# A softmax-weighted causal convolution and a squared-ReLU FFN: the convolution as masked band matmuls on TensorE instead of products on GpSimd and adds on VectorE

## The chip, the cores and the metric

One NeuronCore of a Trainium2 chip runs the whole program. The metric is the device time of one execution in microseconds (us). The engines are TensorE (PE, with its weight loads listed apart as PEld), VectorE (DVE), ScalarE (ACT), GpSimd (POOL) and SyncE (SP), which here only issues DMAs. Each engine takes its own instructions in its own order and waits on semaphores for the others.

## The reference

There are 8 batches of 4096 tokens with 192 channels. Each token has, for each of 8 heads, 7 weights; a softmax over the 7 makes them add up to one. A head owns 24 neighbouring channels, and output token s is the weighted sum of the input tokens s-6 to s (zeros ahead of the batch). The result goes through an FFN of 2048 hidden units.

```
w = exp(weight_gen - max);  w = w / sum(w)              # over the 7 taps
x_pad = 6 rows of zeros, then x                         # per batch
y[b,s,h,g] = sum_k  w[b,s,h,k] * x_pad[b, s+k, h, g]    # h: 8 heads, g: 24 channels
h = maximum(y @ w_in, 0)                                # 192 -> 2048
out = (h * h) @ w_out                                   # 2048 -> 192
```

Inputs and output are f32; inside, both kernels use f16 operands with f32 sums in TensorE.

## The kernel before

The 32768 tokens are cut into 64 blocks of 512 tokens (`TB`), a block into four chunks of 128 tokens, one token to a partition. The loop over `it` is a software pipeline: in one round block `it` loads its inputs, block `it-1` is convolved, block `it-2` transposed, block `it-3` does the first FFN product and block `it-4` the second. The order in which the instructions stand on each engine is set by the framework's scheduler from this program order and from its own estimates of readiness; the rows shown further down are that final order.

- **Load** (`st_dma_in`, L89 to L112, on SP's queue): the weights of the block, and for each chunk a tile `X6` that holds seven shifted copies of the 128 rows, in f32.
- **Softmax** (L117 on ACT, L121 and L124 on DVE, L129 on POOL).
- **Products** (`st_mult`, L140, POOL): one instruction per chunk multiplies the seven shifted copies by their tap weights into `pk`, 1344 elements on each of 128 partitions, f16. `pk` has two buffers, one for each block in flight.
- **Adds** (`st_preadd`, L152, L155, L158, DVE): the seven products are summed in three instructions per chunk.
- **Transposes** (`st_fold_pe`, L169, PE): eight per block turn the sums to channels-by-tokens; ACT copies them out (L179). The 192 channels are held as two groups of 128 that overlap by 64; the overlapping rows of `w_in` are zero in the second group. The first FFN product therefore has two matmuls for each 128 hidden units.
- **First FFN product** (`st_mm1`, L188, 32 matmuls of 128x512 per block), ReLU on ACT (`st_relu`, L204, into `t1`, four buffers), square on DVE (`st_sq`, L209).
- **Second FFN product** (`st_mm2`, L219, 64 matmuls of 192 columns per block), copied out by ACT (L230) and sent by SP (L237).

Of the kernel before, what the change touches and what calls it, by code (L numbers as in the profile page):

```python
# [7 lines left out]


@with_exitstack
def kernel(
# [7 lines left out]
):  # L20
    nc = tc.nc
# [3 lines left out]
    B, S, D = x.shape  # L25
    H, KK = weight_gen.shape[2], weight_gen.shape[3]
    G = D // H
    Dff = moe_w_in.shape[1]
    Dm = moe_w_out.shape[1]
    PAD = KK - 1  # L30
# [3 lines left out]
    NCH = TB // P  # L34
    NBLK_PER_B = S // TB
    NBLK = B * NBLK_PER_B
    NF = Dff // P
    NFP = NF // 2

# [4 lines left out]
    d_chunks = [(0, P), (D - P, P)]  # L44

    const = ctx.enter_context(tc.tile_pool(name="const", bufs=1))

    ident = const.tile([P, P], f16, name="ident")
    make_identity(nc, ident)

    w_in16 = []
    for ci, (dd0, dn) in enumerate(d_chunks):
        t = const.tile([P, Dff], f16, name=f"w_in16_{ci}")
        if ci == 0:
            nc.gpsimd.dma_start(out=t, in_=moe_w_in[dd0 : dd0 + P, :])
        else:
            pad = 2 * P - D
            nc.vector.memset(t[0:pad, :], 0.0)  # L58
            nc.gpsimd.dma_start(out=t[pad:P, :], in_=moe_w_in[dd0 + pad : D, :])
        w_in16.append(t)  # L60

    w_out16 = const.tile([P, NF, Dm], f16, name="w_out16")
    nc.gpsimd.dma_start(  # L63
        out=w_out16, in_=moe_w_out.rearrange("(c p) m -> p c m", p=P)
    )

    p_wg = ctx.enter_context(tc.tile_pool(name="p_wg", bufs=2))
    p_e = ctx.enter_context(tc.tile_pool(name="p_e", bufs=2))
    p_sm = ctx.enter_context(tc.tile_pool(name="p_sm", bufs=2))
    p_nrm = ctx.enter_context(tc.tile_pool(name="p_nrm", bufs=2))  # L70
    p_x6 = ctx.enter_context(tc.tile_pool(name="p_x6", bufs=3))
    p_pk = ctx.enter_context(tc.tile_pool(name="p_pk", bufs=2))
    p_yt = ctx.enter_context(tc.tile_pool(name="p_yt", bufs=2))
    p_t1 = ctx.enter_context(tc.tile_pool(name="p_t1", bufs=4))
    p_g = ctx.enter_context(tc.tile_pool(name="p_g", bufs=2))
    p_os = ctx.enter_context(tc.tile_pool(name="p_os", bufs=3))
    ps_y = ctx.enter_context(tc.tile_pool(name="ps_y", bufs=1, space=bass.MemoryType.PSUM))
    ps_h = ctx.enter_context(tc.tile_pool(name="ps_h", bufs=3, space=bass.MemoryType.PSUM))
    ps_o = ctx.enter_context(tc.tile_pool(name="ps_o", bufs=1, space=bass.MemoryType.PSUM))

    wg_t, e_t, rcp_t, nrm_t, x6_t, pk_t, yt_t, g_t = ({} for _ in range(8))
    t1_t, hps_t, o2_t, osb_t = ({} for _ in range(4))

    def st_dma_in(j):
        b = j // NBLK_PER_B
        t0 = (j % NBLK_PER_B) * TB
        wg = p_wg.tile([P, NCH, H, KK], f32, name="wg")
        wg_t[j] = wg
        nc.sync.dma_start(  # L89
            out=wg,  # L90
            in_=weight_gen[b, t0 : t0 + TB].rearrange("(c p) h k -> p c h k", p=P),
        )
        X6 = p_x6.tile([P, NCH, KK, D], f32, name="X6")
        x6_t[j] = X6
        for c in range(NCH):
            s0 = t0 + c * P
            if s0 == 0:
                nc.vector.memset(X6[0:PAD, c, 0:PAD, :], 0.0)  # L98
                for k in range(KK):
                    tstart = max(0, PAD - k)  # L100
                    nc.sync.dma_start(  # L101
                        out=X6[tstart:P, c, k, :],
                        in_=x[b, 0 : P - PAD + k, :],
                    )
            else:
                base = x[b, s0 - PAD : s0 - PAD + P, :]
                src = bass.AP(
                    tensor=base.tensor,
                    offset=base.offset,
                    ap=[list(base.ap[0]), [D, KK], list(base.ap[1])],  # L110
                )
                nc.sync.dma_start(out=X6[:, c], in_=src)  # L112

    def st_exp(j):
        e = p_e.tile([P, NCH, H, KK], f32, name="e")
        e_t[j] = e
        nc.scalar.activation(out=e, in_=wg_t[j], func=ActF.Exp)  # L117

    def st_sm(j):
        ssum = p_sm.tile([P, NCH, H], f32, name="ssum")  # L120
        nc.vector.tensor_reduce(out=ssum, in_=e_t[j], axis=AxisX, op=AluOp.add)  # L121
        rcp = p_sm.tile([P, NCH, H], f32, name="rcp")
        rcp_t[j] = rcp
        nc.vector.reciprocal(out=rcp, in_=ssum)  # L124

    def st_nrm(j):
        nrm = p_nrm.tile([P, NCH, H, KK], f32, name="nrm")
        nrm_t[j] = nrm
        nc.gpsimd.tensor_tensor(  # L129
            out=nrm,  # L130
            in0=e_t[j],
            in1=rcp_t[j].unsqueeze(-1).broadcast_to((P, NCH, H, KK)),
            op=AluOp.mult,
        )

    def st_mult(j, c):
        if c == 0:
            pk_t[j] = p_pk.tile([P, NCH, KK, H, G], f16, name="pk")
        pk = pk_t[j]
        nc.gpsimd.tensor_tensor(  # L140
            out=pk[:, c],
            in0=x6_t[j][:, c].rearrange("p k (h g) -> p k h g", h=H),
            in1=nrm_t[j][:, c]
            .rearrange("p h k -> p k h")
            .unsqueeze(-1)
            .broadcast_to((P, KK, H, G)),
            op=AluOp.mult,
        )

    def st_preadd(j, c):  # L150
        v = pk_t[j][:, c].rearrange("p k h g -> p k (h g)")
        nc.vector.tensor_tensor(  # L152
            out=v[:, 0:3, :], in0=v[:, 0:3, :], in1=v[:, 4:7, :], op=AluOp.add
        )
        nc.vector.tensor_tensor(  # L155
            out=v[:, 0:2, :], in0=v[:, 0:2, :], in1=v[:, 2:4, :], op=AluOp.add
        )
        nc.vector.tensor_tensor(  # L158
            out=v[:, 0], in0=v[:, 0], in1=v[:, 1], op=AluOp.add
        )  # L160

    def st_fold_pe(j):
        yps = ps_y.tile([P, 2, TB], f16, name="yps")
        yt_t[j] = [yps, None]
        pk = pk_t[j]
        for c in range(NCH):
            y16 = pk[:, c, 0].rearrange("p h g -> p (h g)")
            for ci, (dd0, dn) in enumerate(d_chunks):
                nc.tensor.transpose(  # L169
                    out=yps[:, ci, c * P : (c + 1) * P],  # L170
                    in_=y16[:, dd0 : dd0 + P],
                    identity=ident,
                )

    def st_yt_evac(j):
        yps = yt_t[j][0]
        yt16 = p_yt.tile([P, 2, TB], f16, name="yt16")
        yt_t[j][1] = yt16
        nc.scalar.copy(out=yt16, in_=yps)  # L179

    def st_mm1(j, fp):
        yt16 = yt_t[j][1]
        hps = ps_h.tile([P, 2, TB], f32, name="hps")
        hps_t[(j, fp)] = hps
        for jj in range(2):
            fc = 2 * fp + jj
            for ci, (dd0, dn) in enumerate(d_chunks):
                nc.tensor.matmul(  # L188
                    out=hps[:, jj, :],
                    lhsT=w_in16[ci][:, fc * P : (fc + 1) * P],  # L190
                    rhs=yt16[:, ci, :],
                    start=(ci == 0),
                    stop=(ci == len(d_chunks) - 1),
                )
# [119 lines left out]
```

## Time and profile before

| | |
|---|---|
| device time, median of 2 runs | 1389.86 us (1389.41 to 1390.3) |
| profiled execution, span from first to last instruction | 1387.2 us |
| PE busy / PEld busy | 937.2 us (68%) / 627.6 us (45%) |
| DVE busy | 1070.5 us (77%) |
| ACT busy | 632.5 us (46%) |
| POOL busy | 725.6 us (52%) |
| mean granted TensorE clock | 0.836 of full speed |
| 16 DMA engines, hardware queue q1 | 42.2% |

The profile gives one execution. Its span is 2.7 us shorter than the median of the runs, which also hold what lies ahead of the first and behind the last instruction. Busy shares are averages over the run. A row of the groups view reads: line, engine, operation, output<-input, sizes, count, then busy time and mean duration of one, then the idle time of the engine ahead of these instructions and who ended it. A row of the timeline reads: start, duration of the stretch, engine, line, operation, count, and in brackets the idle time ahead of it. Matmul durations overlap, since they are pipelined; the distance from one start to the next is what a matmul costs in a stream.

### The profile page before, as it was taken

How to read it: one execution, taken by the hardware profiler on the slowest of the kernel's cores; microseconds unless marked ns; L12 is line 12 of the kernel's file. 1: busy time of each engine (PE TensorE's matmuls, PEld its weight loads, DVE VectorE, ACT ScalarE, POOL GpSimd, SP SyncE). 2: the span in 40 equal slices, each digit the busy share in tenths (PEclk: the TensorE clock that was granted, in tenths of full speed). 3: DMA queues.
4: the chain of work that ended last, by engine and by line, in shares of the span. 5: the costliest groups of instructions: out<-in, count | busy, mean ns of one | idle time of the engine just before them, and what ended most of it. 6: DMA issues, size and time to landing. Idle time of an engine off the chain costs nothing.

```text
span 1387.2 us, 17548 instructions
## 1 busy us (share of the span) xinstructions
PE 937.2 (68%) x6656; PEld 627.6 (45%) x6656; DVE 1070.5 (77%) x1417; ACT 632.5 (46%) x769; POOL 725.6 (52%) x329
## 2 busy tenths in 40 slices
PE   0376666766766766767767668668667667677688
PEld 0144443544544544534535435435445445444456
DVE  2989778778787787787787787787887877877863
ACT  0244444544544544444444445445445445444455
POOL 3766545646546546456456455455465465464430
PEclk9888888878888888788788878888888888788899
DMA  8524456554443543444443443544434434434001
GB/s 240 218 101 153 144 194 242 192 176 143 159 179 120 173 177 128 166 143 144 181 161 129 166 167 139 183 149 140 177 137 158 176 119 177 173 107 179 15 24 41
DMA packets 114053, 211.26 MB, mean 152 GB/s; under 512 B 42264, under 2 KB 82032, under 8 KB 113968
## 3 DMA queue, kind: packets, MB, share of 16 engines
q1 hardware_dynamic: 111680, 208.57, 42.2%
q0 software_dynamic: 2288, 1.57, 0.8%
q8 instruction: 52, 0.85, 0.3%
q14 instruction: 33, 0.27, 0.1%
HBM read 186.52 MB, written 25.17 MB: 153 GB/s over the span
## 4 chain that ended last, share of the span: by engine, by line
DVE 52%; PE 25%; POOL 12%; ACT 6%; issue 3%; SPq 1%; DMA 1%; POOLq 0%; ACTq 0%; DVEq 0%
DVE pk L152 17%; DVE pk L155 16%; PE o L219 16%; DVE pk L158 13%; POOL pk L140 12%; PE hps L188 9%; DVE gT L209 5%; ACT t L204 4%; ACT o_sb L230 2%; SPq L112 1%; DMA wg<-in_weight_gen_dram 1%; SPq L101 1%; DVE ssum L121 0%; PE yps L169 0%; DVE rcp L124 0%
## 5 line engine op out<-in xcount | busy, mean ns | idle before, releaser
L140 POOL TENSOR_TENSOR pk<-X,nrm 128x1344 f16<-128x1344 f32 x256 | 672.1, 2655 | 511.5 <-ACT o_sb L230 469.0
L188 PE MATMUL hps<-yt,w_in 128*128 128x512 f16 x2048 | 526.3, 408 | 374.1 <-ACT t L204 373.0
L204 ACT ACTIVATE t<-hps 128x1024 f16<-128x1024 f32 x512 | 489.8, 1028 | 424.7 <-DVE gT L209 403.0
L188 PEld LDWEIGHTS <-w_in 128*128 128x128 f16 x2048 | 206.3, 101 | 620.7 <-issue 425.7
L152 DVE TENSOR_TENSOR pk<-pk 128x576 f16<-128x576 f16 x256 | 264.1, 1032 | 231.6 <-POOL pk L140 231.6
L219 PE MATMUL o<-w_out,gT 128*128 128x192 f16 x4096 | 421.3, 268 | 8.5 <-DVE gT L209 7.3
L219 PEld LDWEIGHTS <-gT 128*128 128x128 f16 x4096 | 395.3, 108 | 65.4 <-issue 45.4
L209 DVE TENSOR_TENSOR gT<-t 128x1024 f16<-128x1024 f16 x512 | 344.4, 711 | 28.3 <-ACT t L204 24.8
L155 DVE TENSOR_TENSOR pk<-pk 128x384 f16<-128x384 f16 x256 | 249.4, 974 | 6.3
L158 DVE TENSOR_TENSOR pk<-pk 128x192 f16<-128x192 f16 x256 | 207.5, 811 | 6.2
L230 ACT COPY o_sb<-o 128x384 f32<-128x384 f32 x128 | 61.2, 478 | 266.4 <-PE o L219 266.4
L129 POOL TENSOR_TENSOR nrm<-e,rcp 128x224 f32<-128x224 f32 x64 | 50.5, 789 | 91.8 <-DVE rcp L124 65.7
L169 PE MATMUL yps<-ident,pk 128*128 128x128 f16 x512 | 42.2, 222 | 63.9 <-DVE pk L158 63.9
L179 ACT COPY yt<-yps 128x1024 f16<-128x1024 f16 x64 | 64.8, 1012 | 31.6 <-PE yps L169 31.6
L169 PEld LDWEIGHTS <-pk 128*128 128x128 f16 x512 | 33.5, 98 | 69.8 <-POOL pk L140 59.0
L121 DVE TENSOR_REDUCE ssum<-e 128x32 f32<-128x224 f32 x64 | 24.2, 377 | 26.0 <-ACT e L117 26.0
L117 ACT ACTIVATE e<-wg 128x224 f32<-128x224 f32 x64 | 24.5, 383 | 28.3 <-DMA wg<-in_weight_gen_dram 28.3
L124 DVE RECIPROCAL rcp<-ssum 128x32 f32<-128x32 f32 x64 | 22.5, 352 | 5.3 <-DVE ssum L121 0.5
L98 DVE MEMSET X<- 6x1152 f32 x8 | 8.1, 1018 | 1.4 <-issue 1.2
L58 DVE MEMSET w_in<- 64x1024 uint32 x1 | 0.9, 912 | 1.0 <-PEq L298 1.0
L117 ACT ACT_TABLE_LOAD x1 | 1.3, 1283 | 0.7 <-PEq L298 0.7
L63 POOL DMA_DIRECT2D w_out<-in_moe_w_out_dram x1 | 1.2, 1208 | 0.0
(8 smaller groups left out, 2.2 us busy)
## 6 DMA issues: line engine op xcount, KB each, us to landing
X<-in_x_dram SPq DMA_DIRECT2D x248, 672.0 KB
out_dram<-o_sb SPq DMA_DIRECT2D x128, 192.0 KB
wg<-in_weight_gen_dram SPq DMA_DIRECT2D x64, 112.0 KB
X<-in_x_dram SPq DMA_DIRECT2D x8, 96.0 KB
w_out<-in_moe_w_out_dram POOLq DMA_DIRECT2D x1, 768.0 KB, 18.3
X<-in_x_dram SPq DMA_DIRECT2D x8, 95.2 KB
X<-in_x_dram SPq DMA_DIRECT2D x8, 94.5 KB
X<-in_x_dram SPq DMA_DIRECT2D x8, 93.8 KB
```

What stands on the lines that cost most here:

```text
L129: nc.gpsimd.tensor_tensor(out=nrm, in0=e_t[j], in1=rcp_t[j].unsqueeze(-1).broadcast_to((P, NCH, H, KK)), op=AluOp.mult,)
L140: nc.gpsimd.tensor_tensor(out=pk[:, c], in0=x6_t[j][:, c].rearrange("p k (h g) -> p k h g", h=H), in1=nrm_t[j][:, c] .rearrange("p h k -> ...
L152: nc.vector.tensor_tensor(out=v[:, 0:3, :], in0=v[:, 0:3, :], in1=v[:, 4:7, :], op=AluOp.add)
L155: nc.vector.tensor_tensor(out=v[:, 0:2, :], in0=v[:, 0:2, :], in1=v[:, 2:4, :], op=AluOp.add)
L158: nc.vector.tensor_tensor(out=v[:, 0], in0=v[:, 0], in1=v[:, 1], op=AluOp.add)
L169: nc.tensor.transpose(out=yps[:, ci, c * P : (c + 1) * P], in_=y16[:, dd0 : dd0 + P], identity=ident,)
L179: nc.scalar.copy(out=yt16, in_=yps)
L188: nc.tensor.matmul(out=hps[:, jj, :], lhsT=w_in16[ci][:, fc * P : (fc + 1) * P], rhs=yt16[:, ci, :], start=(ci == 0), stop=(ci == len(d_ch ...
L204: nc.scalar.activation(out=t1, in_=hps_t[(j, fp)], func=ActF.Relu)
L209: nc.vector.tensor_tensor(out=gT[:, 2 * fp : 2 * fp + 2, :], in0=t1, in1=t1, op=AluOp.mult)
L219: nc.tensor.matmul(out=o2[:, c % 2, :], lhsT=gT[:, fc, c * P : (c + 1) * P], rhs=w_out16[:, fc, :], start=(fc == 0), stop=(fc == NF - 1),)
L230: nc.scalar.copy(out=o_sb, in_=o2_t[(j, half)])
```

## The change

The convolution is rewritten, and with it everything ahead of the FFN. The work is still 64 blocks of 512 tokens.

- **Softmax by batch.** `st_wg_load` loads the weights of a whole batch in one tile, 32 tokens and a halo of 6 to a partition (2128 f32 per partition). `st_softmax` runs one exp on ACT (L135), one reduce (L137), one reciprocal (L139) and five multiplies (L147) on DVE, eight times in all. The multiplies write the rows skewed into one of two tiles `v0`, `v1` (`vbuf`; both are `v_...` in the rows below), so that token t's own 8 slots hold the weights that it takes in the outputs t to t+6. SP writes this to a DRAM tile `vd` (L155).
- **Loads.** For each block five overlapping windows of 128 tokens, 98 apart, are loaded: `xt` (x in f16, converted by the DMA, on POOL's queue) and `wr` (the skewed weights from `vd`, on SP's queue; 64 f16 a row).
- **Bands.** `st_band` (L200, DVE, five per block) multiplies `wr`, repeated along the free axis, by a constant 0/1 mask; the result `bd` is for each head a 128 by 96 to 112 band matrix.
- **Convolution.** `st_conv` (L228, PE) contracts `xt` (as weights) with `bd`: 16 matmuls per window, 80 per block. Each has all 128 rows and up to 32 columns of weights (`tile_position=(0, p0)`, one of four column groups), because a group of 32 channels touches two heads: first with the later head over all 32 channels, then again with the earlier head over its 8, 16 or 24 channels. The output `yp` is already channels-by-tokens. Channels 128 to 191 are written twice, to partitions 0 to 63 and 64 to 127.
- **FFN.** `y` is copied from PSUM by DVE (L241). The first product stays at two matmuls per 128 hidden units: `w_b`'s upper 64 rows are zero (`ROW_TILED` is False). `st_mm2` is issued in eight parts, one behind each of the eight pairs of `st_mm1`. `h` has two PSUM buffers (before: three), `o` two (before: one).
- **Gone:** `X6`, the products on POOL, the adds, the transposes, the identity.

```
+    def st_softmax(b):
+        wg = wg_t[b]
+        v = vbuf[b % 2]
+        nc.scalar.activation(out=wg, in_=wg, func=ActF.Exp)
+        ssum = p_sm.tile([P, RH, H], f32, name="ssum")
+        nc.vector.tensor_reduce(out=ssum, in_=wg, axis=AxisX, op=AluOp.add)
+        rcp = p_sm.tile([P, RH, H], f32, name="rcp")
+        nc.vector.reciprocal(out=rcp, in_=ssum)
+        pp = list(v.ap[0])
+        for i0 in range(0, RH, SL):
+            n = min(SL, RH - i0)
+            vo = bass.AP(
+                tensor=v.tensor, offset=v.offset + i0 * H * SL,
+                ap=[pp, [H * SL + 1, n], [SL, H], [H * SL, KK]],
+            )
+            nc.vector.tensor_tensor(
+                out=vo,
+                in0=wg[:, i0 : i0 + n],
+                in1=rcp[:, i0 : i0 + n].unsqueeze(-1).broadcast_to((P, n, H, KK)),
+                op=AluOp.mult,
+            )
+        vd = p_dr.tile([S, H * SL], f16, name="vd")
...
+    def st_band(j, i):
+        if i == 0:
+            bd_t[j] = p_bd.tile([P, H * TB], f16, name="bd")
+        lo, hi = bounds[i], bounds[i + 1]
+        n = hi - lo
...
+        nc.vector.tensor_tensor(
+            out=bd_t[j][:, H * lo : H * hi].rearrange("p (h m c) -> p h m c", h=H, c=SL),
+            in0=wr_t[j][:, i].unsqueeze(2).broadcast_to((P, H, n // SL, SL)),
+            in1=m.rearrange("p (m c) -> p m c", c=SL)
+            .unsqueeze(1)
+            .broadcast_to((P, H, n // SL, SL)),
+            op=AluOp.mult,
+        )
...
+    def st_conv(j):
+        yp = ps_y.tile([P, 2, TB], f32, name="yp")
...
+        for i in range(NT):
+            lo, hi = bounds[i], bounds[i + 1]
+            bd = bd_t[j][:, H * lo : H * hi].rearrange("p (h c) -> p h c", h=H)
+            for later in (True, False):
+                for q, ci, p0 in places:
+                    _, ha, hb, pre = quads[q]
+                    m = 32 if later else pre
+                    nc.tensor.matmul(
+                        out=yp[p0 : p0 + m, ci, lo:hi],
+                        lhsT=x_t[j][:, i, 32 * q : 32 * q + m],
+                        rhs=bd[:, hb if later else ha, :],
+                        start=True,
+                        stop=True,
+                        skip_group_check=True,
+                        tile_position=(0, p0),
                     )
...
+        st_softmax(0)
+        st_load(0)
+        load_weights()
+        st_load(1)
+        st_load(2)
+        for i in range(NT):
+            st_band(0, i)
+        st_conv(0)
+        st_y_evac(0)
+        for j in range(NBLK + 1):
+            nb = j // NBB + 1
+            if j < NBLK and nb < B:
+                if j % NBB == 0:
+                    st_wg_load(nb)
+                if j % NBB == 2:
+                    st_softmax(nb)
+            if j + 3 < NBLK:
+                st_load(j + 3)
+            for fp in range(NFP):
+                if j < NBLK:
+                    st_mm1(j, fp)
+                    st_relu(j, fp)
+                if j >= 1:
+                    st_mm2(j - 1, fp)
+                if j < NBLK:
+                    if j + 1 < NBLK:
+                        if fp < NT:
+                            st_band(j + 1, fp)
+                        if fp == NT:
+                            st_conv(j + 1)
+                            st_y_evac(j + 1)
+                    st_sq(j, fp)
```

How the instructions stand on PE. Before, in the middle of the run, the transposes of a block (L169, reading `pk`) stand between two halves of the second FFN product (L219) and the first matmul of the next block's first product (L188):

```order
L219 MATMUL o_5526<-w_out_68,gT 128x192
L169 LDWEIGHTS pk [waits Pool_49]
L169 MATMUL yps<-ident,pk 128x128
L169 LDWEIGHTS pk
L169 MATMUL yps<-ident,pk 128x128
```

Now, at the same point of a block, the last of the 80 convolution matmuls (L228) is followed directly by the next pair of the first product (L249 and L254); ahead of the convolution stands a part of the second product:

```order
L228 MATMUL yp<-bd,xt 8x112
L228 LDWEIGHTS xt
L228 MATMUL yp<-bd,xt 16x112
L228 LDWEIGHTS xt
L228 MATMUL yp<-bd,xt 8x112
L249 LDWEIGHTS w_a
L249 MATMUL h<-y,w_a 128x512 [waits Activation_49]
L254 LDWEIGHTS w_b
L254 MATMUL h<-y,w_b 128x512
```

The eight transposes are gone, 80 narrow matmuls with a weight load each have come, and the two FFN products alternate in eighths.

How they stand on DVE, in the middle of the run. Before, each chunk's three adds wait for POOL's product, and the squares (L209) stand among and behind them:

```order
L152 TENSOR_TENSOR pk<-pk 128x576 [waits Pool_49]
L209 TENSOR_TENSOR gT<-t_5637 128x1024 [waits Activation_49]
L155 TENSOR_TENSOR pk<-pk 128x384 [waits DVE_49]
L209 TENSOR_TENSOR gT<-t_5644 128x1024 [waits Activation_49]
L158 TENSOR_TENSOR pk<-pk 128x192 [waits DVE_49]
L209 TENSOR_TENSOR gT<-t_5656 128x1024 [waits Activation_49]
L209 TENSOR_TENSOR gT<-t_5664 128x1024 [waits Activation_49]
```

Now there is no wait for POOL; the copy of `yp` (L241) waits for the convolution of block j+1, and behind it come the bands (L200) of block j+2 and the last two squares (L279) of block j:

```order
L279 TENSOR_TENSOR g<-t_6073 128x1024 [waits Activation_49]
L241 CAST y<-yp 128x1024 [waits PE_49]
L200 TENSOR_TENSOR bd<-wr,mask 128x832 [waits DMAHW3_49,DVE_49]
L200 TENSOR_TENSOR bd<-wr,mask 128x832
L279 TENSOR_TENSOR g<-t_6172 128x1024 [waits Activation_49]
L200 TENSOR_TENSOR bd<-wr,mask 128x768 x2
L279 TENSOR_TENSOR g<-t_6188 128x1024 [waits Activation_49]
L200 TENSOR_TENSOR bd<-wr,mask 128x896
```

The scheduler has moved the bands a whole block ahead of the convolution that reads them.

At the start of the program DVE now begins with the softmaxes of the first two batches, interleaved (`v_101` is the first batch, `v_102` the second):

```order
L308 MEMSET v_101 128x1408
L308 MEMSET v_102 128x1408
L102 MEMSET w_b 64x1024
L137 TENSOR_REDUCE ssum<-wg 128x304 [waits DMAHW0_49,Activation_49]
L137 TENSOR_REDUCE ssum<-wg 128x304 [waits DMAHW1_49,Activation_49]
L139 RECIPROCAL rcp<-ssum 128x304 [waits DVE_49] x2
L147 TENSOR_TENSOR v_101<-wg,rcp 128x8x8x7 [waits DVE_49]
L147 TENSOR_TENSOR v_102<-wg,rcp 128x8x8x7 [waits DVE_49]
```

The softmax of the second batch, written in the third round of the loop, now stands ahead of the first band; those of the other six batches stand among the first ten or so blocks.

More of the change, by code (lines that the diff above doesn't have):

```diff
@@ L6 @@
 from concourse import bass_utils, mybir
-from concourse.masks import make_identity
 from concourse._compat import with_exitstack
+ROW_TILED = False
 @with_exitstack
@@ L114, in st_exp @@
[L114 to L132, printed above, removed]
+            out=vd.rearrange("(p r) c -> p (r c)", p=P),
@@ L162, in st_fold_pe @@
[L162 to L179, printed above, removed]
+    G = D // H
```

322 lines of the change are left out of this document (161 added, 161 removed).

## The prediction

> **What bounds the kernel now.** I read the page first (busy shares, slices, chain), then the timeline of one block in the middle, then the same lines at the end of the run.
>
> ```profile
> core 0: 1387.2 us, clock 0.836
> PE 937.2 (68%) x6656; PEld 627.6 (45%) x6656; DVE 1070.5 (77%) x1417; ACT 632.5 (46%) x769; POOL 725.6 (52%) x329
> DVE 52%; PE 25%; POOL 12%; ACT 6%; issue 3%; SPq 1%; DMA 1%; POOLq 0%; ACTq 0%; DVEq 0%
> L140 POOL TENSOR_TENSOR pk<-X,nrm 128x1344 f16<-128x1344 f32 x256 | 672.1, 2655 | 511.5 <-ACT o_sb L230 469.0
> ```
>
> No engine is full, and the chain is half DVE's. The timeline of one block in the middle shows why (start, duration, engine, line, count, idle time ahead):
>
> ```profile
> 605.72 10.45 POOL L140 TENSOR_TENSOR pk<-X,nrm 128x1344 f16<-128x1344 f32 x4 [9.56 <-ACT o_sb L230]
> 608.31 2.80 DVE L152 TENSOR_TENSOR pk<-pk 128x576 f16<-128x576 f16 x1 [4.05 <-POOL pk L140]
> 611.14 2.60 DVE L155 TENSOR_TENSOR pk<-pk 128x384 f16<-128x384 f16 x1
> 613.78 2.50 DVE L158 TENSOR_TENSOR pk<-pk 128x192 f16<-128x192 f16 x1
> 616.21 0.45 DVE L152 TENSOR_TENSOR pk<-pk 128x576 f16<-128x576 f16 x1
> 619.71 1.94 ACT L204 ACTIVATE t<-hps 128x1024 f16<-128x1024 f32 x2 [6.70 <-DVE gT L209]
> 620.41 0.25 DVE L158 TENSOR_TENSOR pk<-pk 128x192 f16<-128x192 f16 x1
> 620.79 1.86 PE L188 MATMUL hps<-yt,w_in 128*128 128x512 f16 x4 [6.40 <-ACT t L204]
> 621.78 3.62 DVE L209 TENSOR_TENSOR gT<-t 128x1024 f16<-128x1024 f16 x6
> 625.74 0.61 PE L169 MATMUL yps<-ident,pk 128*128 128x128 f16 x8
> 626.43 10.46 POOL L140 TENSOR_TENSOR pk<-X,nrm 128x1344 f16<-128x1344 f32 x4 [9.34 <-ACT o_sb L230]
> ```
>
> A block takes 626.43 - 605.72 = 20.7 us. While POOL multiplies, a DVE add lasts about as long as a POOL product: 2.80, 2.60 and 2.50 us, against 0.45 and 0.25 us for the same instructions once POOL has stopped at 616.2. Squares queue behind these adds, the ReLUs wait 6.70 us for `t1` buffers, PE waits 6.40 us for the ReLUs. POOL's next block then starts 0.08 us behind the end of the transposes that free its `pk` buffer (the bracket names an ACT copy that feeds no product). So the block's period is a ring through four engines.
>
> The ring does not bind at the end, where POOL is out of work. Windows there and in the middle (length, busy time by engine, granted clock, DMA share, GB/s), and the timeline:
>
> ```profile
> 600.00:700.00 100.00, 72.78 (x520) 48.82 (x519) 78.53 (x100) 48.11 (x59) 55.43 (x24) 0.83 0.43 151
> 1336.00:1376.00 40.00, 40.00 (x327) 28.38 (x326) 17.80 (x27) 28.15 (x34) 0.00 (x0) 0.99 0.10 31
> ...
> 1351.80 0.25 PE L219 MATMUL o<-w_out,gT 128*128 128x192 f16 x1
> 1352.33 0.38 PE L188 MATMUL hps<-yt,w_in 128*128 128x512 f16 x1
> 1352.61 2.80 PE L219 MATMUL o<-w_out,gT 128*128 128x192 f16 x32
> 1355.25 6.86 PE L188 MATMUL hps<-yt,w_in 128*128 128x512 f16 x31
> 1356.10 7.44 ACT L204 ACTIVATE t<-hps 128x1024 f16<-128x1024 f32 x8 [0.17 <-PE hps L188]
> ```
>
> With PE never idle the granted clock is 0.99; in the middle, with 6.4 us of idle per block, it is 0.83. So PE loses twice: the wait, and a slower clock behind it.
>
> **The change, part by part.** All of POOL's 672.1 us and the adds go, and with them the ring. What is late next? I compare the engines per block.
>
> *PE, FFN.* At full clock, start to start: a 512-column matmul (6.86 - 0.38)/30 = 0.216 us, a 192-column one (2.80 - 0.25)/31 = 0.082 us. So 32 x 0.216 + 64 x 0.082 = 6.91 + 5.27 = 12.2 us per block. The padding of K costs nothing new: there were two matmuls per 128 hidden units before.
>
> *PE, convolution.* 80 matmuls of 96 to 112 columns (mean 102.4) with 32 or fewer columns of weights. The trace has no such shape. The nearest row is the transposes of 128 columns:
>
> ```profile
> L169 PE MATMUL yps<-ident,pk 128*128 128x128 f16 x512 | 42.2, 222 | 63.9 <-DVE pk L158 63.9
> L169 PEld LDWEIGHTS <-pk 128*128 128x128 f16 x512 | 33.5, 98 | 69.8 <-POOL pk L140 59.0
> ```
>
> Eight in 0.61 us, the last lasting 0.22: (0.61 - 0.22)/7 = 0.056 us apart, each with a weight load of 98 ns hidden beside its neighbours. From 0.216 at 512 columns and 0.056 at 128, a column costs 0.417 ns; 102.4 columns then cost 0.045 us, and 80 of them **3.6 us** per block. Ends: the four column groups side by side, a quarter, 0.9 us; each matmul with an unhidden weight load, 0.045 + 0.098 = 0.143 us, 11.4 us. I take 3.6, since the transposes, also a load per matmul, lie on that line.
>
> The Trainium skill, "TensorEngine Tiling (Array Packing)", section "Key Properties", says that a change of tiling mode drains TensorE. No row here shows it. As an estimate by that page, two drains of some 0.16 us (0.22 - 0.056) per block would add about 21 us to the run.
>
> *PE in all:* 12.2 + 3.6 = **15.8 us** per block.
>
> *DVE.* The rows that price it, with those of ACT:
>
> ```profile
> L209 DVE TENSOR_TENSOR gT<-t 128x1024 f16<-128x1024 f16 x512 | 344.4, 711 | 28.3 <-ACT t L204 24.8
> L179 ACT COPY yt<-yps 128x1024 f16<-128x1024 f16 x64 | 64.8, 1012 | 31.6 <-PE yps L169 31.6
> L230 ACT COPY o_sb<-o 128x384 f32<-128x384 f32 x128 | 61.2, 478 | 266.4 <-PE o L219 266.4
> L121 DVE TENSOR_REDUCE ssum<-e 128x32 f32<-128x224 f32 x64 | 24.2, 377 | 26.0 <-ACT e L117 26.0
> L117 ACT ACTIVATE e<-wg 128x224 f32<-128x224 f32 x64 | 24.5, 383 | 28.3 <-DMA wg<-in_weight_gen_dram 28.3
> L124 DVE RECIPROCAL rcp<-ssum 128x32 f32<-128x32 f32 x64 | 22.5, 352 | 5.3 <-DVE ssum L121 0.5
> ```
>
> Squares, 8 x 3.62/6 = 4.8 us. The copy of `yp`, 1024 f32 from PSUM, was ACT's at 1.01 us; between 0.7 (L209) and 1.7 (L121 scaled up) I take 1.2. Bands: 4096 f16 elements in five instructions; from 0.25 us at 192 and 0.45 at 576, 832 cost 0.58, so 2.9 us; at worst twice that if the repeated operand halves the rate, 5.8. Sum 8.9, at worst 11.8, under PE's 15.8.
>
> Softmax, per batch: reduce of 2128 at most 9.5 x 0.377 = 3.6, I take 2.4 (part of 0.377 is fixed); reciprocal of 304 at most 9.5 x 0.352 = 3.3, I take 2.6; five multiplies of up to 448 near 0.6 each. About 8 us, and exp some 1.9 us on ACT (0.383 at 224, 1.0 at 1024). Since the order puts bands a block ahead of their convolution, a softmax among the squares is covered by DVE's slack of 6.9 us per block, except where a long instruction holds back a square: I book 8 us in all, between 0 and 6 x 5 = 30. Without the cover, with bands just ahead, each would cost about 3 to 5 us.
>
> *ACT:* 8 x 7.44/8 + 2 x 0.48 = 8.4 us. Covered.
>
> *DMA and queues.*
>
> ```profile
> q1 hardware_dynamic: 111680, 208.57, 42.2%
> q0 software_dynamic: 2288, 1.57, 0.8%
> L63 POOL DMA_DIRECT2D w_out<-in_moe_w_out_dram x1 | 1.2, 1208 | 0.0
> ```
>
> A packet took 0.422 x 16 x 1387.2/111680 = 0.084 us of one engine. A block now moves 640 rows of x, 640 of `wr`, 512 of output and a share of the batch loads, some 1830 packets: 1830 x 0.084/16 = 9.6 us, under 15.8 and prefetched three blocks ahead. POOL issues one x load per block, at most 1.2 us each by L63.
>
> *Head and tail.* Before, the first weights, 112 KB, came 2.3 us after issue, and the span ended 3.4 us behind the start of the last copy:
>
> ```profile
> 0.75 0.44 SPq L89 DMA_DIRECT2D wg<-in_weight_gen_dram  x1
> 3.07 0.39 ACT L117 ACTIVATE e<-wg 128x224 f32<-128x224 f32 x1 [1.05 <-DMA wg<-in_weight_gen_dram]
> 0.00:37.00 37.00, 0.37 (x2) 0.14 (x2) 9.64 (x10) 2.06 (x3) 14.72 (x16) 1.00 0.88 251
> ...
> 1383.78 0.48 ACT L230 COPY o_sb<-o 128x384 f32<-128x384 f32 x1 [2.89 <-PE o L219]
> ```
>
> Now 1.09 MB at 251 GB/s plus latency, landed at 6.5; exp to 8.5; two interleaved softmaxes on DVE, 16 us, to 24.7; `vd` written by 28.5, read back by 31; bands and a cold convolution (twice 3.6) to 38.5; the copy, 40 us. Between 33 and 48.
>
> *Sum.* 40 + 64 x 12.2 + 63 x 3.6 + 8 + tail 4 = 40 + 781 + 227 + 8 + 4 = **1060 us** span; with the 2.7 us by which the median exceeds the profiled span, 1063.
>
> **Rivals.**
>
> 1. *Column groups run side by side.* Nothing in the trace speaks for or against it. Convolution 0.9 to 2.0 us instead of 3.6: 63 x 1.6 to 2.7 less, 890 to 960 us. The Trainium skill, "TensorE: Matmul & The Clock Gate", section "Part 3: Packing small matmuls", gives 2.38 times for three column tiles of 512 columns; as an estimate by that ratio the convolution would be about 1.5 us, and the run near 930.
> 2. *Weight loads are not hidden.* With 32-column loads, a quarter of 98 ns exposed: 0.070 us per matmul, 5.6 us, +126: near 1190. With the full 98 ns exposed: 11.4 us, +490, **1555 us, slower than before**. It decides from (1418 - 1063)/63 = 5.6 us more per block, that is 0.115 us per matmul. Against it: every load in the trace hides (0.056 apart with 98 ns loads). The Trainium skill, "TensorEngine Tiling (Array Packing)", section "Restrictions", says that column tiling switches off Fast Weight Load, which speaks for a dearer load per column; the narrower weights speak against it.
> 3. *Bands at half rate.* Behind the convolution DVE has the copy 1.2, three or four bands at 1.15 and two squares before PE's second part of `st_mm2` needs the last square; that is about 0.9 us late per block, +57: 1120.
> 4. *The clock does not recover.* If PE's sustained load were granted 0.836 as now: 1008/0.836 adds 198, 1260. Against it: 0.99 over the 40 us at the end.
>
> **How the numbers follow.** A change within 2% of 1390 could not be told from none. Chances: forecast 0.50 (own range 1015 to 1115), column groups 0.20, quarter load 0.14, full load 0.04, bands 0.07, clock 0.05. The predicted time is the likeliest case's, 1063. The range 920 to 1195 keeps the forecast, most of rival 1, the quarter load and the bands; out are the full load, the clock and the cheapest part of rival 1. Faster by over 2%: 0.93; slower by over 2%: 0.04; within 0.03.
>
> **What would show it.** Right: PE's row near 9 in all slices and PEclk 9 throughout; block period near 15.8; L228 0.045 us start to start; L200 near 0.6 us; POOL almost idle; first L249 near 40 us. Wrong: idle time on PE ended by DVE (bands, rival 3) or by SP's queue; L228 far from 0.045 either way; PEclk at 8 with PE full; idle time ahead of the convolution that `xt` ended, since POOL's queue then can't keep up.

## The result, and the profile after

The changed kernel takes **960.58 us** (960.44 to 960.71, 2 runs) against 1389.86 us: ratio 0.691, 95% interval 0.689 to 0.693. The forecast was 1063 us with a range of 920 to 1195, so sign and range held; the point lay 102 us too high. The profiled execution has a span of 958.7 us.

The page of the changed kernel: busy time, granted clock by slices, and the chain that ended last.

```profile
span 958.7 us, 25454 instructions
PE 866.7 (90%) x11264; PEld 598.9 (62%) x11264; DVE 685.0 (71%) x956; ACT 587.1 (61%) x649; POOL 64.4 (7%) x97
PE   0196746799999999999999999999999999999998
PEclk9998888799999999999999999999999999999999
PE 80%; DVE 15%; DMA 3%; issue 1%; ACT 1%; SPq 0%; ACTq 0%; DVEq 0%
```

PE has taken DVE's place as the bound, but only from the ninth of 40 slices on; its steady pace begins at 214 us. In the five slices ahead of that, from 72 us on, it is 4 to 7 tenths busy, at a clock of 7 or 8 tenths. The two regimes, as windows (length, busy time by engine, granted clock, DMA share, GB/s):

```profile
48.00:210.00 162.00, 119.40 (x1383) 76.60 (x1383) 154.26 (x164) 82.01 (x86) 7.28 (x9) 0.87 0.35 83
302.00:402.00 100.00, 100.00 (x1360) 69.81 (x1359) 66.50 (x104) 66.94 (x75) 6.50 (x9) 1.00 0.30 54
```

In the second, PE is busy for all 100 us at clock 1.00. In the first, DVE is: 154.26 of 162 us. The convolution in the steady part, as a timeline:

```profile
507.01 1.09 PE L228 MATMUL yp<-bd,xt 128*32 128x104 f16 x80
508.03 0.39 PE L249 MATMUL h<-y,w_a 128*128 128x512 f16 x1
508.26 0.38 PE L254 MATMUL h<-y,w_b 128*128 128x512 f16 x1
```

From the first convolution matmul to the next product are 508.03 - 507.01 = 1.02 us for 80 matmuls, where the prediction had 3.6. The convolution of each block starts 13.31 us behind the last one, in every block from 214.2 us on, against 20.7 us in the block of the old kernel that the prediction shows. With 12.2 us of FFN in it, 1.1 us are left for the convolution: 1.02 and a further 0.09 ahead of it (section on e6).

Of the groups, the multiplies of the softmax are the surprise; and the wait that they cause stands in the row of the first product:

```profile
L147 DVE TENSOR_TENSOR v<-wg,rcp 128x448 f16<-128x448 f32 (+1 forms) x40 | 80.0, 2146 | 0.1
L249 PE MATMUL h<-y,w_a 128*128 128x512 f16 x1024 | 393.4, 384 | 44.3 <-DVE y L241 37.4
```

A multiply takes 2.146 us in the mean of four with 448 elements (2.25 us each) and a last one with 336 (1.71); the prediction's price was 0.6. The timeline of the costliest wait shows how it reaches PE:

```profile
94.76 6.04 DVE L147 TENSOR_TENSOR v<-wg,rcp 128x448 f16<-128x448 f32 x3
98.76 1.98 ACT L135 ACTIVATE wg<-wg 128x2128 f32<-128x2128 f32 x1 [10.19 <-DMA wg<-in_weight_gen_dram]
100.42 1.43 DVE L241 CAST y<-yp 128x1024 f16<-128x1024 f32 x1
101.91 0.61 PE L249 MATMUL h<-y,w_a 128*128 128x512 f16 x1 [14.11 <-DVE y L241]
```

DVE takes its instructions in order: the copy of `yp` stands behind the multiplies, and PE waits 14.11 us for it. At the same time an exp that waits 10.19 us for its load blocks the ReLUs behind it on ACT.

**The span in four terms**, all from starts of L228: head to the first convolution 43.4; 63 periods of 13.31 = 838.5; a loss of 51, since the nine blocks from 43.4 to 214.2 us took 170.8 instead of 9 x 13.31 = 119.8 (six of the eight softmaxes run in them; the first two lie in the head); and 25.8 behind the last convolution. Sum 958.7. The experiments ask what makes the 13.31 and what the 51.

### The profile page after: what moved, and what is told of

Same layout as the page of the kernel before. It is cut to its first block, busy times and chain, and to the rows that moved or that the text cites. A ratio compares the mean times of both kernels' runs of the same rounds, so it can differ in the third digit from the quotient of the medians.

```text
span 958.7 us, 25454 instructions
## 1 busy us (share of the span) xinstructions
PE 866.7 (90%) x11264; PEld 598.9 (62%) x11264; DVE 685.0 (71%) x956; ACT 587.1 (61%) x649; POOL 64.4 (7%) x97
## 4 chain that ended last, share of the span: by engine, by line
PE 80%; DVE 15%; DMA 3%; issue 1%; ACT 1%; SPq 0%; ACTq 0%; DVEq 0%
PE o L289 32%; PE h L249 21%; PE h L254 21%; DVE v L147 8%; PE yp L228 6%; DVE g L279 3%; DMA wg<-in_weight_gen_dram 2%; DVE bd L200 2%; DVE rcp L139 1%; DVE ssum L137 1%; DVE y L241 1%; DMA wr<-vd 1%; ACT t L273 0%; DMA vd<-v 0%; ACT wg L135 0%
## 5 line engine op out<-in xcount | busy, mean ns | idle before, releaser
L273 ACT ACTIVATE t<-h 128x1024 f16<-128x1024 f32 x512 | 523.1, 1023 | 305.6 <-PE h L254 289.4
L279 DVE TENSOR_TENSOR g<-t 128x1024 f16<-128x1024 f16 x512 | 353.8, 693 | 252.7 <-ACT t L273 252.6
L249 PE MATMUL h<-y,w_a 128*128 128x512 f16 x1024 | 393.4, 384 | 44.3 <-DVE y L241 37.4
L289 PEld LDWEIGHTS <-g 128*128 128x128 f16 x4096 | 355.9, 98 | 122.3 <-issue 3.5
L289 PE MATMUL o<-w_o,g 128*128 128x192 f16 x4096 | 424.1, 247 | 0.3 <-DVE g L279 0.2
L254 PE MATMUL h<-y,w_b 128*128 128x512 f16 x1024 | 392.7, 383 | 0.0
L200 DVE TENSOR_TENSOR bd<-wr,mask 128x832 f16<-128x832 f16 (+2 forms) x320 | 173.3, 576 | 6.8 <-DMA wr<-vd 6.8
L249 PEld LDWEIGHTS <-w_a 128*128 128x128 f16 x1024 | 100.8, 98 | 107.9 <-DVE y L241 38.3
L254 PEld LDWEIGHTS <-w_b 128*128 128x128 f16 x1024 | 101.1, 99 | 70.1 <-issue 10.6
L228 PE MATMUL yp<-bd,xt 128*32 128x104 f16 (+7 forms) x5120 | 71.8, 211 | 43.4 <-DVE bd L200 43.4
L228 PEld LDWEIGHTS <-xt 128*32 128x32 f16 (+3 forms) x5120 | 60.0, 94 | 55.3 <-issue 45.9
L147 DVE TENSOR_TENSOR v<-wg,rcp 128x448 f16<-128x448 f32 (+1 forms) x40 | 80.0, 2146 | 0.1
L241 DVE CAST y<-yp 128x1024 f16<-128x1024 f32 x64 | 79.1, 1237 | 0.0
L135 ACT ACTIVATE wg<-wg 128x2128 f32<-128x2128 f32 x8 | 15.8, 1978 | 57.5 <-DMA wg<-in_weight_gen_dram 57.5
L137 DVE TENSOR_REDUCE ssum<-wg 128x304 f32<-128x2128 f32 x8 | 18.8, 2345 | 4.1 <-ACT wg L135 4.1
L139 DVE RECIPROCAL rcp<-ssum 128x304 f32<-128x304 f32 x8 | 16.1, 2021 | 0.0
L188 POOL DMA_DIRECT2D xt<-in_x_dram x8 | 6.0, 751 | 0.0
```

The lines of the kernel that those rows point to most:

```text
L137: nc.vector.tensor_reduce(out=ssum, in_=wg, axis=AxisX, op=AluOp.add)
L147: nc.vector.tensor_tensor(out=vo, in0=wg[:, i0 : i0 + n], in1=rcp[:, i0 : i0 + n].unsqueeze(-1).broadcast_to((P, n, H, KK)), op=AluOp.mult,)
L200: nc.vector.tensor_tensor(out=bd_t[j][:, H * lo : H * hi].rearrange("p (h m c) -> p h m c", h=H, c=SL), in0=wr_t[j][:, i].unsqueeze(2).bro ...
L228: nc.tensor.matmul(out=yp[p0 : p0 + m, ci, lo:hi], lhsT=x_t[j][:, i, 32 * q : 32 * q + m], rhs=bd[:, hb if later else ha, :], start=True, ...
L241: nc.vector.tensor_copy(out=y, in_=yp_t[j])
L249: nc.tensor.matmul(out=h[:, jj, :], lhsT=w_a[:, fc * P : (fc + 1) * P], rhs=y[:, 0, :], start=True, stop=False,)
```

## The experiments

All ratios are to the kernel before on the same chip, with 95% intervals; its medians there were 1389.38 to 1390.72 us.

### Why the convolution is cheap: e1, e5

e1 issues the matmuls of each window column group by column group:

```
-            for later in (True, False):
-                for q, ci, p0 in places:
+            for q, ci, p0 in sorted(places, key=lambda t: t[2]):
+                for later in (True, False):
```

> The changed kernel with the 16 convolution matmuls of each window in another order: the four matmuls of one column group stand together, instead of the four groups in turn. Same matmuls, same count, same result. Theory A (four column groups in turn run side by side, which is why 80 matmuls took 1.02 us): in this order neighbours mostly share a group and come one behind the other, some 0.045 us each, so the convolution takes near 3.6 us, a block 13.3 + 2.6 = 15.9 us, and the run 960.6 + 63 x 2.6 = about 1120 us, less if the two groups at a border still overlap. Theory B (narrow matmuls are cheap in any order, 0.012 us each): the convolution stays at 1.0 us and the run at 960 us.

Measured: 968.01 us, 0.6965 (0.6954 to 0.6977), period 13.40, and the stretch of 80 lasts hardly longer:

```profile
511.91 1.18 PE L228 MATMUL yp<-bd,xt 128*32 128x104 f16 x80
```

This doesn't decide, and the expectation of theory A was wrong, because it took for granted that matmuls start in program order. In the trace they don't: the first matmuls of the four groups start 13 to 14 ns one behind the other, ahead of matmuls that stand earlier in the program but belong to a busy group. (The starts in the trace come with 32, 32, 32, 32, then 24, 16, 8, 24 columns of weights; in the program the second matmul has 24.) In program order, each group's fourth would start 3 x 0.045 us behind its first and hold back the next group, 20 x 3 x 0.045 = 2.7 us in all; it took 1.18. The Trainium skill, "TensorE: Matmul & The Clock Gate", section "The mechanism", says that matmuls start and end strictly in program order; for matmuls of different column groups this run shows otherwise.

e5 takes the groups themselves away:

```
-        yp = ps_y.tile([P, 2, TB], f32, name="yp")
+        yp = yp_one                    # one tile, zeroed once
-        places = [(q, 0, 32 * q) for q in range(4)]
-        places += [(q, 1, 32 * (q - 4)) for q in (4, 5)]
-        places += [(q, 1, 32 * (q - 2)) for q in (4, 5)]
+        places = [(q, 0, 0) for q in range(4)]
+        places += [(q, 1, 0) for q in (4, 5)]
+        places += [(q, 1, 0) for q in (4, 5)]
```

> The same 80 convolution matmuls per block, with the same shapes, weights and bands, but all in the first column group (partitions 0 to 31); yp is one tile, zeroed once, and what the other partitions should hold is left out. Theory A, the four column groups run side by side, each one a 104-column matmul per 45 ns: in one group the stretch of 80 becomes 80 x 0.045 = 3.6 us instead of 1.02, the block period 13.31 + 2.6 = 15.9 us, the run 960 + 64 x 2.6 = about 1125 us. Theory B, a narrow matmul is simply cheap (11 to 13 ns), wherever it writes: the stretch stays near 1.02 us, the run near 960. Theory C, the load of the 32 weights is not hidden when the next matmul goes to the same group: more than 45 ns, up to 45 + 98 = 143 ns each, 11.4 us per block and a run near 1620.

Measured: 1125.42 us, 0.8097 (0.8081 to 0.8114); period 16.01 us.

```profile
503.14 3.79 PE L231 MATMUL yp<-bd,xt 128*32 128x104 f16 x80
506.86 0.39 PE L252 MATMUL h<-y,w_a 128*128 128x512 f16 x1
```

The same 80 matmuls now take 3.72 us, 42, 46 and 49 ns from start to start for 96, 104 and 112 columns. That is theory A. That the run meets its 1125 us to the microsecond is luck: the period came 0.1 us longer than forecast, and the loss of the first blocks smaller (44 us, reckoned as above, instead of 51). The serial price of the prediction, 0.045 us, was right; four groups run side by side and divide it by 3.72/1.02 = 3.6. C is out: the 32-column loads, 93 ns each (98 for 128 columns), don't add to the 45 ns of the matmuls. The Trainium skill, "TensorE: Matmul & The Clock Gate", section "Part 3: Packing small matmuls — row/col tiling", has 2.38 times for three column tiles at 512 columns; the trace has 3.6 for four at 104, with the gap behind the last matmul that the next section looks at.

### What a change of tiling mode costs: e6

`ROW_TILED = True`: the second K part of two neighbouring groups of hidden units in two row halves.

> ROW_TILED is set: the 64 rows of the second K part are used in two halves, so that the second matmuls of two neighbouring groups of hidden units stand in two row halves of TensorE and could run side by side. T1, side by side, with a switch of tiling mode into and out of each of the 8 pairs that costs about as much as around the convolution (0.23 us): 8 x (0.216 - 0.23) = nothing gained, 960 us. T2, side by side with no cost of the switch: 8 x 0.216 = 1.7 us less per block, 13.31 - 1.73 = 11.6, about 850 us. T3, the two halves don't overlap: 960 without a cost of the switch, 960 + 64 x 8 x 0.23 = 1078 with it. My choice is T1, 950 to 985.

Measured: 958.12 us, 0.6893 (0.6881 to 0.6904); period 13.28.

```profile
500.98 0.59 PE L249 MATMUL h<-y,w_a 128*128 128x512 f16 x2
501.51 0.39 PE L262 MATMUL h<-y,w_b 64*128 64x512 f16 x2
501.83 0.83 PE L289 MATMUL o<-w_o,g 128*128 128x192 f16 x8
```

This is T1. The two half-height matmuls start 4 ns apart, so they do overlap and save 0.216 us. But the switch in costs 311 - 216 = 95 ns and the one out 318 - 216 = 102 ns (from the start of the second L249 to that of L262, 501.51 - 500.98 - 0.216, and from L262 to L289, where a 512-column matmul's 216 ns would do): 0.197 of 0.216 us is lost, and the period falls by 0.03 us only. The same switches stand around the convolution in the changed kernel: 176 instead of 82 ns into it, and 145 ns from its last matmul to L249, where the price of a matmul is 11 ns side by side and 45 serial. That is 0.19 to 0.23 us per block, or, as an estimate, 12 to 15 us per run. The Trainium skill, "TensorEngine Tiling (Array Packing)", section "Key Properties", names a drain at a change of mode; the trace has a gap at each, of the size given here.

### What makes the multiply slow: e2, e3, e7, e8

Four forms of the multiply's write. e2 writes `v` dense; e3 turns the order of writing so that neighbouring writes are 16 bytes apart; e7 holds `v` in f32 and lets the DMA on POOL's queue convert it; e8 writes a dense tile on DVE and lets ACT copy it to the skewed places.

```
 e2: ap=[pp, [H * KK, n], [KK, H], [1, KK]]
 e3: ap=[pp, [H * SL + 1, n], [H * SL, KK], [SL, H]]     # inputs turned alike
 e7: vbuf = [const.tile([P, RH + KK - 1, H, SL], f32, ...)]
     nc.gpsimd.dma_start(out=vd..., in_=v...)            # was nc.sync, v in f16
 e8: nc.vector.tensor_tensor(out=wn[:, 0:n], ...)        # dense
     nc.scalar.copy(out=vo, in_=wn[:, 0:n])              # skewed
```

> The changed kernel with the softmax multiplies (L147) writing their f16 results in one dense run instead of the skewed rows, so the convolution's weights are in the wrong places; everything else is the same. Theory A (the 2.15 us of one such multiply come from its scattered writes, 2 bytes at a step of 128): it falls to 0.5 to 0.7 us, the first matmul comes at about 33 us instead of 43, DVE is no longer full between 50 and 210 us, and the run is 35 to 60 us shorter, 900 to 925 us. Theory B (the price is that of f32 inputs with a repeated operand): 2.15 us stays, and the run at 960 us.

> The changed kernel with the same softmax multiplies walking their elements in another order: the 8 heads innermost (writes at a step of 16 bytes, reads of the exponentials at 28 bytes) instead of the 7 taps (writes at a step of 128 bytes, dense reads). Same values in the same places. Theory A1 (the large step of the writes is what costs): near 0.6 us each, the run 35 to 60 us shorter. Theory A2 (any write that is not dense costs the same): 2.1 us stays, 960 us. Theory B (the repeated f32 operand costs): 2.1 us stays too, and the flat run tells A2 from B.

> The skewed tile v is f32 instead of f16, so that the five multiplies scatter 4-byte values; the write to vd goes to POOL's queue and is converted by the DMA. If scattering 2-byte values is what makes the multiply take 2.15 us, it falls to the dense one's 0.59 us, a softmax from about 15 to 7 us on DVE, and the run to that of the dense kernel, 923 us (918 to 935). If any write that isn't dense costs this, whatever its size, it stays at 2.15 us and the run at 960.

> The multiply writes a dense f16 tile on DVE, and ACT copies it into the skewed places. DVE's part falls to 0.59 us per multiply as in the dense kernel. If the slow write belongs to DVE alone, the copy takes ACT about 0.5 to 0.6 us (its exp moves 2128 elements in 1.98 us) and the run comes to 925 to 935. If ACT's scattered write is as slow as DVE's (2.15 us), 10.7 us per batch move to ACT among the ReLUs that PE waits for, and the run stays at 950 to 970.

| | run, us | ratio | first convolution, us |
|---|---|---|---|
| e2 dense f16 | 923.16 | 0.6645 (0.6629 to 0.6662) | 27.6 |
| e3 f16, 16 bytes apart | 960.19 | 0.6911 (0.6901 to 0.6921) | 43.5 |
| e7 scattered f32 | 939.47 | 0.6759 (0.6749 to 0.6769) | 38.6 |
| e8 dense f16, skewed by ACT | 963.03 | 0.6929 (0.6913 to 0.6945) | 46.3 |

The rows of the writing instruction, in the same order:

```profile
L147 DVE TENSOR_TENSOR v<-wg,rcp 128x448 f16<-128x448 f32 (+1 forms) x40 | 21.9, 593 | 0.0
```

```profile
L147 DVE TENSOR_TENSOR v<-wg,rcp 128x448 f16<-128x448 f32 (+1 forms) x40 | 79.8, 2139 | 0.1
```

```profile
L147 DVE TENSOR_TENSOR v<-wg,rcp 128x448 f32<-128x448 f32 (+1 forms) x40 | 35.2, 928 | 0.2
```

```profile
L154 ACT COPY v<-wn 128x448 f16<-128x448 f16 (+1 forms) x40 | 83.7, 2104 | 12.9 <-DVE wn L148 12.2
```

The second figure behind the count, in ns, is the mean over the four instructions of 448 elements and the one of 336. Scattered 2-byte values cost 2.1 us, on DVE and on ACT alike, and whatever the distance (here 16 or 128 bytes); 4-byte values at the same places of the tile (256 bytes apart) cost 0.93; dense 2-byte values 0.59, the price that the prediction had. So it is the write of single 2-byte values, not DVE and not the stride. e2 came out as theory A has it, e3 as A2, and e8 as its second case.

e7 fell short of its forecast (918 to 935), and its dearer multiply explains little of that. Of the 16.3 us between e7 and e2, 11.0 lie in the head. There the ten multiplies end only 2.5 us later; the write to `vd`, now on POOL's queue, starts 4.75 us later, since in e7 the multiplies of the two batches alternate and in e2 the first batch's five stand first, and takes 10.98 us where e2's takes 4.61. The two rows, from the chain that ended last, e7's first:

```profile
24.22 10.98 DMA vd<-v
```

```profile
19.47 4.61 DMA vd<-v
```

In e11 (next section), with the same f32 tile and queue but one softmax in the head, the same write takes 4.85 us, so the conversion by itself isn't what costs; why the write took 10.98 us in e7 was not tested.

The Trainium skill, "SBUF — State Buffer", section "Door 1: The DMA port swizzle", says that every access that crosses into a new 16-byte line pays; by that alone the f32 form, which crosses as often, should be as slow as the f16 one, and it isn't.

But e2, with cheap multiplies, still loses 31 us in its first eight blocks (137.5 us from 27.6 to 165.1, against 8 x 13.31). Something else is in the 51. e2's list of waits names it (what PE waited for: us in total, times, longest):

```profile
PE h L249 <- ACT t L273: 22.3, 5, 9.0
PE h L249 <- DVE y L241: 5.1, 4, 2.0
```

PE now waits for ReLUs, and hardly for the copy of `y`. The ReLUs stand on ACT behind an exp that itself waits for its load; four of the exps wait 2.91 to 8.76 us. Such a load needs a tile, of which there are two, and is issued only behind the multiplies that free it: at 96.49 us behind those that end at 96.08, with the exp at 105.83.

### What the rest of the loss is: e4, e10, e11

e4 ties the loads of batches 3 to 8 to the block that should come with them, by a one-element DVE write. e10 ties also the exp of all batches but the first to the copy of `y` two blocks later. e11 is e10 with the f32 `v` of e7.

```
 e4, e10, e11, ahead of st_wg_load(nb), nb >= 2:
+  nc.vector.tensor_tensor(out=wg_t[nb - 2][:, 0, 0, 0:1],
+      in0=y_t[j][:, 0, 0:1], in1=y_t[j][:, 0, 1:2], op=AluOp.add)
 e10, e11, ahead of st_softmax(nb):
+  nc.vector.tensor_tensor(out=zt, in0=y_t[j][:, 0, 0:1], in1=zero, op=AluOp.mult)
+  nc.vector.tensor_tensor(out=wg_t[nb][:, 0, 0, 0:1],
+      in0=wg_t[nb][:, 0, 0, 0:1], in1=zt, op=AluOp.add)
```

> The changed kernel with the loads of the softmax weights of batches 3 to 8 held back until the block at which the program asks for them, by a one-element DVE write that depends on that block's y; the multiplies keep their 2.15 us. Six softmaxes then stand among blocks 8 to 50, one per eight blocks, instead of all in the first nine. Theory A (the 51 us lost between 43 and 214 us come from six softmaxes crowded on DVE, 15 us each against a slack of some 4.4 us per block): spread out, each loses at most a few us, the blocks between 43 and 110 us run at 13.3 us, and the run is 20 to 45 us shorter, 915 to 940 us. Theory B (each softmax costs its stall wherever it stands, since a 2 us instruction holds back squares and the copy of y): the loss of 51 us is only spread, 960 us.

> The changed kernel, v still f16; the load of batch 3's weights and the later ones is tied to block 8, 16 and so on, and every exp but the first to the copy of y two blocks later (a one-element DVE write each), so that no exp can stand ahead of its DMA among the ReLUs and only one batch's softmax falls into eight blocks. The slow multiplies (2.15 us) stay. If the loss of the first blocks is bunching and the exp's waits, the head falls by one batch's softmax (about 15 us of DVE, first conv at 30 instead of 43 us), and the 51 us of loss to 7 softmaxes x 5 us = 35: run about 930 (918 to 940). If the slow multiplies alone are the loss, 945 to 960.

> Both edits together: v in f32 (0.93 us per multiply) and the paced softmaxes. The first conv at about 29 us, and 7 softmaxes that cost 2 to 3 us each on top of 64 x 13.31 us: 29 + 5 + 64 x 13.31 + 20 + tail 13 = about 918 us. If the two edits remove the same loss, it is not below 930; if they add, the run is 960 - 21 (the f32 edit alone) - the gain of the paced f16 kernel.

Measured: e4 957.13 us, 0.6894 (0.688 to 0.6908), against 915 to 940 by its theory A: the loss was only spread, as theory B has it. e10 961.36 us, 0.6912 (0.6902 to 0.6922): no gain, against my forecast of 930. e11 **908.91 us**, 0.6536 (0.6525 to 0.6547), below the forecast of about 918, and the fastest kernel of the study.

e10's one softmax per eight blocks can be read alone. A timeline of one in e10, then the same place in e11:

```profile
189.96 2.16 DVE L151 TENSOR_TENSOR v<-wg,rcp 128x448 f16<-128x448 f32 x1
191.72 0.92 DVE L283 TENSOR_TENSOR g<-t 128x1024 f16<-128x1024 f16 x1
192.53 1.66 DVE L151 TENSOR_TENSOR v<-wg,rcp 128x336 f16<-128x336 f32 x1
193.79 1.45 DVE L245 CAST y<-yp 128x1024 f16<-128x1024 f32 x1
195.29 0.61 PE L253 MATMUL h<-y,w_a 128*128 128x512 f16 x1 [7.40 <-DVE y L245]
```

```profile
178.21 0.96 DVE L151 TENSOR_TENSOR v<-wg,rcp 128x448 f32<-128x448 f32 x1
179.00 0.69 DVE L283 TENSOR_TENSOR g<-t 128x1024 f16<-128x1024 f16 x1
179.61 0.75 DVE L151 TENSOR_TENSOR v<-wg,rcp 128x336 f32<-128x336 f32 x1
180.19 1.21 DVE L245 CAST y<-yp 128x1024 f16<-128x1024 f32 x1
181.46 0.39 PE L253 MATMUL h<-y,w_a 128*128 128x512 f16 x1 [1.77 <-DVE y L245]
```

With slow multiplies the copy of `y` comes so late that PE waits 7.40 us, and the block with the one ahead of it takes 23.02 + 13.79 us: a softmax costs 36.81 - 2 x 13.31 = 10.2 us (9.6 to 10.8 over the run). With f32 it is 15.25 + 13.79 - 26.62 = 2.4 us. And the clock follows. Windows of these two blocks:

```profile
183.70:206.70 23.00, 15.60 (x181) 10.13 (x184) 18.58 (x22) 8.91 (x11) 0.84 (x1) 0.85 0.26 60
```

```profile
175.50:190.70 15.20, 13.43 (x177) 9.18 (x176) 12.86 (x20) 8.88 (x11) 1.42 (x2) 1.00 0.49 90
```

In e10 the granted clock falls to 0.85 in the disturbed block, in e11 it stays at 1.00. So pacing gave e10 a head of 28.0 us instead of 43.4, and took it back in seven softmaxes of about 9.9 us; the whole loss, reckoned as above, is 934.0 - 28.0 - 838.5 = 67 us instead of 51. In e4 a softmax cost 5.6 to 6.8 us, spread over three blocks (14.3, 16.42 and 14.85 us for the first). But the last batch's came 39 us behind the seventh's instead of 112, and cost 25. Most of that is the other wait, an exp that stands ahead of its load:

```profile
641.24 1.98 ACT L135 ACTIVATE wg<-wg 128x2128 f32<-128x2128 f32 x1 [15.58 <-DMA wg<-in_weight_gen_dram]
644.17 0.58 PE L249 MATMUL h<-y,w_a 128*128 128x512 f16 x1 [14.96 <-ACT t L273]
```

So the loss has two causes, and the waits of PE's first product tell them apart (us in total over the run; the loss is reckoned as above):

| | waits for the copy of `y` | waits for a ReLU | loss |
|---|---|---|---|
| changed kernel | 37.4 | 6.9 | 51 |
| e2 dense f16 | 5.1 | 22.3 | 31 |
| e7 scattered f32 | 11.5 | 18.1 | 35 |
| e4 loads paced | 11.6 | 20.7 | 51 |
| e10 loads and exps paced | 53.8 | 2.2 | 67 |
| e11 paced, f32 | 14.5 | 2.2 | 16 |

(e4 has a further 13.7 us of waits for squares. The slower clock behind a wait comes on top.) A cheaper write shortens the wait for the copy and leaves the wait for the ReLUs; tying the exps removes the second, and with the slow write the first grows. f32 alone took 21 us off the run, pacing alone nothing, both 52. Why a softmax costs 10 us in e10's order and 6 in e4's is not shown.

### What bound the kernel before: e9

e9 is the kernel before, with POOL's product for two taps only.

```
-            out=pk[:, c],
-            in0=x6_t[j][:, c].rearrange(...),
+            out=pk[:, c, 0:2],                 # pk: two fixed tiles, zeroed once
+            in0=x6_t[j][:, c, 0:2].rearrange(...),
```

> The kernel before, with POOL's products only for two of the seven taps (the other five products are left out; pk is two fixed tiles zeroed once); the adds, the transposes and everything else stay. POOL's share of a block falls from 10.5 to about 3 us, and with it the time in which a DVE add lasts as long as a POOL product. Theory ring: the block's period is the ring POOL products, slowed adds, transposes, pk buffers; without it the adds take 0.25 to 0.45 us and the period falls from 20.7 us to what PE or the adds' own chain needs, 12.7 to 14 us, the run to 860 to 950 us, as fast as the changed kernel. Rival: the adds and their order on DVE set the period by themselves, POOL only happens to run beside them: the run stays above 1250 us.

Measured: 920.69 us, 0.6622 (0.6608 to 0.6635).

```profile
L144 POOL TENSOR_TENSOR pk<-X,nrm 128x384 f16<-128x384 f32 x256 | 240.7, 968 | 472.6 <-PE yps L173 428.4
L156 DVE TENSOR_TENSOR pk<-pk 128x576 f16<-128x576 f16 x256 | 183.7, 750 | 88.0 <-POOL pk L144 87.9
302.00:402.00 100.00, 94.97 (x745) 63.19 (x744) 83.89 (x166) 70.62 (x90) 30.68 (x36) 1.00 0.70 242
```

(The last row is a window of the middle.) The period falls from 20.7 to 13.69 us, and PE's clock rises from 0.83 to 1.00. So POOL's products, and the adds that they slow, were the ring; the adds by themselves don't hold PE back. e9 shortens both at once and doesn't tell which weighed more. (The adds became cheaper, but not to the expected 0.25 to 0.45 us: the first of the three takes 0.75 in the mean, against 1.03 before.) The 470 us that e9 takes off are more than the whole gain of the change, 429 us. With five of seven products left out, e9 is no kernel to use; but its period is the longer one, 13.69 against 13.31, so what it has over the changed kernel lies in the head and the first blocks.

## Why the prediction was right, and where it wasn't

- **The ring before, and PE as the bound after: right.** e9 shows the first; PE at 100 of 100 us in the window 302 to 402 the second, though only from 214 us on. The FFN's 12.2 us is what is left of 13.31 when the convolution's 1.1 is taken off.
- **"I take 3.6, since the transposes, also a load per matmul, lie on that line": the step that failed most.** The serial price held (3.72 us in e5). What failed was to take a serial neighbour, with 128 columns of weights, as the nearest row for matmuls in four column groups. Rival 1, at 0.20, was the case: 1.12 us with the switches, 63 x (3.6 - 1.12) = 156 us too much.
- **"five multiplies of up to 448 near 0.6 each": wrong by 3.6 times.** A dense one takes 0.593; the skewed f16 write takes 2.146.
- **"I book 8 us in all, between 0 and 6 x 5 = 30": wrong, 51.** DVE's work per block was as forecast (bands 0.576 us each, the copy 1.237). But the slack of 6.9 us was worked out from a block of 15.8 us; with 13.31 it is 13.31 - 8.9 = 4.4. It was gone in the first nine blocks, where six softmaxes are bunched (154.26 of 162 us busy). And the prediction looked only at squares that a long instruction holds back: what PE waited for was the copy of `y` behind the multiplies, and ReLUs behind an exp whose load had not landed.
- **Head 40: the first L249 came at 48.0.** Two interleaved softmaxes, 16 us by the sum, with 19 us for the ten multiplies alone.
- **Rivals 2, 3, 4: no.** Loads hide (e5); bands run at 0.576 us, where the full rate was priced at 0.58; the clock recovers to 1.00.

The sum by the measured terms: 1060 - 156 + 43 + 8 = 955, against a span of 958.7. Two errors of opposite sign, 156 and 51, made the forecast look better than its terms. Even the range held by luck: with the convolution alone put right, the forecast would have been 1063 - 156 = 907, below its lower end of 920. The longer head and the loss of the first blocks brought the time back into it.

## What to carry to other kernels

Here a small matmul's price was a serial price divided by the column groups it was spread over, plus a fixed price for each change of tiling mode; both are read from the starts, not the durations. Look at how an instruction writes before you take its price from its element count. And where work comes in bursts, ask which in-order engine has both the burst and the instruction that the bound engine waits for: e11 gained 52 us on the changed kernel by a cheaper write (21 alone) and a later start (nothing alone).

## What the runs showed of the hardware that I had not expected

- Matmuls of four column groups start 2 to 4 ns apart in the changed kernel, and ahead of earlier ones of a busy group in e1.
- Single 2-byte writes cost 5.0 ns per element on DVE, what is fixed per instruction included (2146/426; a softmax's five instructions hold 4 x 448 + 336 elements, 426 on average) and 4.9 on ACT, dense ones 1.4 (593/426), scattered 4-byte ones 2.2 (928/426).
- A change of tiling mode cost 95 ns in one direction and 102 in the other (e6).
